# Scatter ahead of the own half, and ranks ahead of sums and x row, in eight steps of a fused attention and mixture-of-experts kernel

## The chip, the cores and the metric

The kernel runs on one core of a Trainium2 chip. The metric is the time of one execution in device microseconds; smaller is better. The core has the engines TensorE (PE in the profile, its weight loads as PEld), VectorE (DVE), ScalarE (ACT), GpSimd (POOL) and SyncE (SP), each with a queue of its own that is worked through in program order. They meet by semaphores.

## The reference

Windowed causal attention over 8 batches, 8 heads, 576 positions and 64 features is followed by a mixture of 8 experts, of which each token takes the one with the largest logit.

```python
scores = scale * np.matmul(q, k.transpose(0, 1, 3, 2))
mask = (rel >= 0) & (rel < 64)               # rel: query position - key position
scores = np.where(mask, scores, -1000000000.0)
attn = softmax(scores)                       # written out, with 1e-09 in the divisor
x = (attn @ v).transpose(0, 2, 1, 3).reshape(4608, 512)

logits = (x / |x|) @ (emb / |emb|).T / tau   # norms with 1e-06 added
expert_idx = np.argmax(logits, axis=1)
gate_w = softmax(logits)[arange(N), expert_idx]
for e in range(8):
    h = np.maximum(x[mask_e] @ w1[e], 0.0)   # 512 -> 1024
    out[mask_e] = gate_w * (h @ w2[e])       # 1024 -> 512
```

## The kernel before

The 4608 tokens are 36 tiles of 128 rows. A tile T holds two blocks of 64 positions for all heads. The order of all instructions is written out by hand. `stages(s)` (L580) writes step s of a software pipeline, and a loop calls it for s = 0 to 34; the last tile is written out behind it and is interleaved with the first expert's work.

In step s different tiles are in different states, and each engine works through its own part in this order:

- TensorE: `scores(s)` into the PSUM tile `score` (L255), in some steps the logits of four tiles (`logits_four`, L403), `values_other(s-2)` (L321), the transposes of the attention weights of tile s-1 (`attn_transposes`, L285), the transposes of x of tile s-3 (L378), in some steps the ranks of four tiles (`ranks`), and `values_mine(s-2)` (L335).
- ScalarE: `own_scores(s)` copies one half of the scores out (L262); in some steps half a weight tile is rounded to w1h (L599); `attn_copy(s-1)` (L295); the copy of x's transposes (L384); in some steps the copies of logits (L413, L416); squares; and at the end `exponentials(s)` (L276).
- VectorE: `all_scores(s)` (L265), `maxima(s)` (L269), in some steps the choice of the expert (L445 to L449), `attn_prev(s-1)` (L298), in some steps `rank_own` (L503), `x_out(s-2)`, which is sums, reciprocal and the x row (L359, L360, L363), then `ranks_out` (a reduction to the rows' places `pi`, L513), and in some steps the weight difference w1l = w1raw - w1h of 512 columns (L686).
- GpSimd: `less_max(s)` subtracts the maxima (L273), in some steps tokens and counts (L367, L457), `attn_own(s-1)` multiplies the own half of the attention weights with its mask (L301), and `place(T)` scatters the rows of a tile to the DRAM table `xs` at the places `pi` (an indirect DMA, L522).

`values_mine(s-2)` in step s reads what `attn_own(s-2)` wrote in step s-1. `scores(s+1)` may begin when `all_scores(s)` has read the PSUM tile.

Tiles come in groups of four (tiles 0 to 27) and of two. The ranks of a group of four that ends before tile b are worked out in step b+5, its tile T is scattered in step T+9. The weight difference is made in the eight steps of `wsplit`: 14, 17, 18, 21, 22, 25, 26 and 29. In 17, 21, 25 and 29 of these a group's ranks fall due, and the scatter of that step needs them. In the other four the places are known from the step before.

After step 30 SyncE's queue loads the first rows of `xs` for the experts (`load_x`, L899); VectorE transposes them in steps 32 and 33 (`x_turned`, L914), behind the x row of that step. From then on the experts' matmuls (L1032, L1093) follow one another on TensorE. There the weight differences are made at L201, x's at L930, and the output rows are scattered at L1121.

Of the kernel before, what the change touches and what calls it, by code (L numbers as in the profile page):

```python
# [33 lines left out]
GROUPS = [(t, t + 4) for t in range(0, 28, 4)] + [(t, t + 2) for t in range(28, 36, 2)]  # L34
# [90 lines left out]
def attention_moe(ctx, tc, q, k, v, emb, tau, w1, w2, kc, kt, out):  # L125
# [14 lines left out]
    def weave(*chains):  # L140

        chains = list(chains)
        while chains:
            chains = [c for c in chains if next(c, chains) is not chains]
# [83 lines left out]
    def scores(T):  # L228

        for z in range(2):  # L230
            if (2 * T + z) % NB == 0:
                for hp in range(2):
                    o = score[64 * z:64 * z + 64, hp].rearrange("p (u c) -> p u c", u=4)[:, :, :WIN]
                    nc.tensor.matmul(o, lhsT=ones[64 * hp:64 * hp + 64, :64],
                                     rhs=low[64 * hp:64 * hp + 64].rearrange("p (u c) -> p u c", u=4),
                                     start=True, stop=True)
        at = T % RK * KT
        for u in range(4):
            for hp, z in sides:
                pr, o = slice(64 * hp, 64 * hp + 64), score[64 * z:64 * z + 64, hp, u * P:(u + 1) * P]  # L240
                qz = qT[pr, T % RQ, u, z * WIN:(z + 1) * WIN]
                own = kT[pr, at + u * P + z * WIN:at + u * P + (z + 1) * WIN]
                if (2 * T + z) % NB == 0:
                    parts = [(o[:, WIN:], own)]
                elif z:
                    parts = [(o, kT[pr, at + u * P:at + (u + 1) * P])]
                else:
                    was = (T - 1) % RK * KT + u * P + WIN
                    if at:
                        hop = KT - WIN  # L250
                        parts = [(o, kT[pr, was:was + 2 * hop].rearrange("p (a c) -> p a c", a=2)[:, :, :WIN])]
                    else:
                        parts = [(o[:, :WIN], kT[pr, was:was + WIN]), (o[:, WIN:], own)]
                for to, keys in parts:
                    nc.tensor.matmul(to, lhsT=qz, rhs=keys, start=True, stop=True)  # L255
# [4 lines left out]
    def own_scores(T):  # L260
        sm[T] = ap.tile([P, 4, 2, WIN], F32, name="sm", bufs=3)
        nc.scalar.copy(sm[T], sv[:, :, :, 1])  # L262
# [17 lines left out]
    def attn_transposes(T):  # L280

        pT[T] = back.rearrange("p (u c) -> p u c", u=4)
        t = sm.pop(T).rearrange("p u h c -> p u (h c)")
        for u in range(4):
            nc.tensor.transpose(pT[T][:, u], t[:, u], ident)  # L285
# [7 lines left out]
    def attn_copy(T):  # L293
        aM[T] = ap.tile([P, 2, 4, P], F32, name="aM", bufs=2)
        nc.scalar.copy(aM[T][:, 0], pT[T])  # L295
# [4 lines left out]
    def attn_own(T):  # L300
        nc.gpsimd.tensor_tensor(out=aM[T][:, 0], in0=aM[T][:, 0], in1=halves[:, 0].unsqueeze(1).to_broadcast([P, 4, P]), op=ALU.mult)  # L301
# [197 lines left out]
    def rank_own(G):  # L499
        a, b = GROUPS[G]  # L500
        n = b - a
        rk = rkb[G] = ap.tile([P, n, E], F32, name="rk")
        nc.vector.tensor_tensor(out=rk, in0=rank.pop(G), in1=ohs.pop(G), op=ALU.mult)  # L503

    def rank_rows(G):
        a, b = GROUPS[G]
        n = b - a
        if G not in rkb:
            rank_own(G)
            yield  # L510
        rks[G] = ap.tile([P, n], I32, name="pi")
        with nc.allow_low_precision("whole numbers"):
            nc.vector.reduce_sum(out=rks[G], in_=rkb.pop(G), axis=AX.X)  # L513
        yield

    def ranks_out(G):
        weave(rank_rows(G))

    def place(T):

        i = T - GROUPS[OF[T]][0]
        d = nc.gpsimd.indirect_dma_start(  # L522
            out=xs[:, :], out_offset=bass.IndirectOffsetOnAxis(ap=rks[OF[T]][:, i:i + 1], axis=0),
            in_=xr.pop(T), in_offset=None, bounds_check=TBL - 1, oob_is_err=False)
        d = getattr(d, "ins", d)
        for o in firsts:
            tc.declare_no_dep(d, o, reason="later tokens' places are behind the early slots")
        for o in puts:
            tc.declare_no_dep(d, o, reason="no two tokens share a place")
        puts.append(d)  # L530
# [42 lines left out]
    wsplit = {s0: (i // 2, slice(i % 2 * 512, i % 2 * 512 + 512)) for i, s0 in enumerate((14, 17, 18, 21, 22, 25, 26, 29))}  # L573

    def warm(n, to=back):

        for _ in range(n):
            nc.tensor.matmul(to[:, :P], lhsT=ones, rhs=ones, start=True, stop=True)

    def stages(s):  # L580

        def there(d):
            return 0 <= s - d < NT

        def ending(d):
            return [G for G, (a, b) in enumerate(GROUPS) if b + d == s]

        def turned():
            if there(1):
                attn_transposes(s - 1)  # L590
                attn_copy(s - 1)

        scores(s)
        if s < 3:
            warm(12, side[1])
        own_scores(s)
        if s in wsplit:
            c, at = wsplit[s]
            nc.scalar.copy(w1h[c][:, at], w1raw[c][:, at])  # L599
        if 0 < s <= 3:  # L600
            exponentials(s - 1)
        if s == 33:
            x_hi(0)
        four = [G for G in ending(3) if len(range(*GROUPS[G])) == 4]
        for G in four:
            logits_four(G)
            four_copy(G)
        load_q(s + RQ)
        if there(2):
            values_other(s - 2)  # L610
        load_v(s + RV - 3)
        for f in wsteps.get(s, ()):
            f()
        if s > 3:
            turned()
        if there(3):
            x_transposes(s - 3)
        for G in four:
            four_back(G)
        if s - 4 in (28, 29):  # L620
            logits(s - 4, side[(s + 1) % 2][:, :E])
        due = [G for G, (a, b) in enumerate(GROUPS) if s == (b + 5 if b - a == 4 else b + 4)]
        for G in due:
            if len(range(*GROUPS[G])) == 4:
                ranks(G)
        if there(2):
            values_mine(s - 2)
        all_scores(s)
        maxima(s)
        late = [G for G in ending(4) if len(range(*GROUPS[G])) == 4]  # L630
        for G in late:
            choose(G)
        if s < 3:
            warm(12, side[1])
        if there(3):
            xT_evac(s - 3)
        for G in four:
            four_out(G)
        if s - 4 in (28, 29):
            nc.scalar.copy(x_rows(s - 4, s - 3)[:, 0, C_LOG:C_LOG + E], side[(s + 1) % 2][:, :E])  # L640
        less_max(s)
        if there(3):
            squares(s - 3)
        for G in four:
            four_beside(G)
        load_k(s + RK - 1, nc.sync if s < 6 else nc.scalar)
        for G in late:
            tokens(G)
            count(G)
        if s > 3:  # L650
            attn_prev(s - 1)
            attn_own(s - 1)
        for G in due:
            if len(range(*GROUPS[G])) == 4:
                rank_own(G)
        if there(2):
            x_out(s - 2)
        if s in (32, 33):
            x_turned(s - 32)
        if 0 < s <= 3:  # L660
            turned()
            attn_prev(s - 1)
            attn_own(s - 1)
        for G in due:
            if len(range(*GROUPS[G])) == 2:
                ranks(G)
            ranks_out(G)
        for G, (a, b) in enumerate(GROUPS):
            for T in range(a, b):
                if s == (T + 9 if b - a == 4 else b + 4):  # L670
                    place(T)
        if s == 33:
            x_lo(0)
        for G in ending(3):
            if len(range(*GROUPS[G])) == 2:
                choose(G)
                tokens(G)
                count(G)
        if s > 2:
            exponentials(s)  # L680
        if s == 33:
            x_hi(1)
            x_lo(1)
        if s in wsplit:
            c, at = wsplit[s]
            nc.vector.tensor_tensor(out=w1l[c][:, at], in0=w1raw[c][:, at], in1=w1h[c][:, at].bitcast(F32), op=ALU.subtract)  # L686
        if 1 <= s < 7:
            blanks(s - 1)
# [588 lines left out]
    T, G = NT - 1, len(GROUPS) - 1  # L1277
# [201 lines left out]
```

## Time and profile before

| | |
|---|---|
| Median of 3 runs | 608.63 us (607.76 to 610.57) |
| Profiled execution | 604.64 us, its span 602.9 us |
| TensorE busy | 580.4 us, 96% of the span |
| VectorE busy | 368.3 us, 61% |
| ScalarE busy | 292.8 us, 49% |
| GpSimd busy | 243.0 us, 40% |
| Granted TensorE clock, mean | 0.996 |
| Bytes moved | 110.11 MB, mean 183 GB/s |

Times in the rows are microseconds from the start of the span. In a timeline row stand the start, the duration, the engine, the line of the kernel, the operation, what it writes and reads, and in brackets the idle time ahead of it on its engine with what ended that. Consecutive instructions of an engine overlap by up to about 0.1 us at their ends, so a start of the next one may lie ahead of the end of the last. TensorE's ends are modelled.

### The profile page before, as it was taken

The page shows a single profiled execution, that of the slowest core. Times are in us where ns is not written, and L with a number is a line of the kernel's source. Part 1 is how long each engine was busy: PE and PEld are TensorE (multiplying, and loading weights), DVE is VectorE, ACT ScalarE, POOL GpSimd, SP SyncE. Part 2 cuts the span into 40 slices and gives each one's busy share as a digit, 9 for nine tenths or more (in the row PEclk, how much of TensorE's full clock was granted, in tenths as well). Part 3 has the DMA queues.
Part 4 walks back from the last instruction along what each step waited for, and adds up shares of the span by engine and source line. Part 5 has one row for each costly group of instructions (what it writes and reads, how often), then busy time and mean ns, then how long its engine had stood idle before and what let it go on. Part 6 is the DMA issues. An engine that isn't in the chain of part 4 may idle for free.

```text
span 602.9 us, 16141 instructions
## 1 busy us (share of the span) xinstructions
PE 580.4 (96%) x6198; PEld 500.2 (83%) x6198; DVE 368.3 (61%) x880; ACT 292.8 (49%) x519; POOL 243.0 (40%) x230
## 2 busy tenths in 40 slices
PE   8998899999999999999999999999999999999995
PEld 7887788788889888888888888888888999989984
DVE  5787889988589766166066166156255473728583
ACT  3676777777441465155145145235344363436362
POOL 3657878887822433314215115105204233113221
PEclk9999999999999999999999999999999999999998
DMA  8988889886334787743544454445336355556820
GB/s 282 301 257 268 285 258 297 262 274 189 136 112 173 206 273 221 201 126 126 168 148 127 138 151 157 110 155 184 89 122 207 117 158 144 177 177 174 241 91 23
DMA packets 72471, 110.11 MB, mean 183 GB/s; under 512 B 14773, under 2 KB 34997, under 8 KB 72384
## 3 DMA queue, kind: packets, MB, share of 16 engines
q1 hardware_dynamic: 62080, 80.88, 46.0%
q0 software_dynamic: 6000, 19.18, 8.2%
q10 hardware_dynamic: 4304, 8.93, 4.6%
q8 instruction: 50, 0.82, 0.6%
q14 instruction: 37, 0.30, 0.1%
HBM read 89.69 MB, written 20.05 MB: 182 GB/s over the span
## 4 chain that ended last, share of the span: by engine, by line
PE 76%; DVE 7%; issue 6%; DMA 3%; POOL 3%; ACT 2%; SPq 0%; POOLq 0%; ACTq 0%; DVEq 0%
PE ph L1032 35%; PE po L1093 33%; DMA out<-o,rest 2%; DVE sm L265 2%; DVE aM L298 2%; PE back L285 1%; POOL sm L273 1%; PE odd L335 1%; PE score L255 1%; POOL aM L301 1%; PE odd L321 1%; DVE st L269 1%; PE even L335 1%; PE xback L378 1%; ACT sm L262 1%
## 5 line engine op out<-in xcount | busy, mean ns | idle before, releaser
L1053 DVE SCALAR_TENSOR_TENSOR hl<-ph,hh 128x512 fp32r<-128x512 f32 (+2 forms) x84 | 54.2, 648 | 154.6 <-ACT hh L1049 154.6
L1032 PE MATMUL ph<-xh,w1h 128*128 128x512 f32 (+2 forms) x384 | 132.7, 345 | 1.3 <-DVE rk L503 1.3
L1032 PE MATMUL ph<-xl,w1h 128*128 128x512 f32 (+2 forms) x384 | 132.1, 344 | 0.0
L1032 PE MATMUL ph<-xh,w1l 128*128 128x512 f32 (+2 forms) x384 | 132.1, 344 | 0.0
L930 POOL TENSOR_TENSOR xl<-xt,xh 128x512 fp32r<-128x512 f32 x37 | 61.7, 1668 | 166.1 <-ACT xh L926 165.8
L1093 PE MATMUL po<-w2l,hh 128*128 128x512 f32 x312 | 121.8, 390 | 0.6 <-DVE w2l L201 0.5
L1093 PE MATMUL po<-w2h,hh 128*128 128x512 f32 x312 | 122.0, 391 | 0.0
L1093 PE MATMUL po<-w2h,hl 128*128 128x512 f32 x312 | 121.7, 390 | 0.0
L1049 ACT ACTIVATE hh<-ph 128x512 fp32r<-128x512 f32 (+2 forms) x84 | 47.4, 566 | 133.2 <-PE ph L1032 121.6
L1121 POOL DMA_INDIRECT out<-o,rest x39 | 43.0, 1101 | 132.3 <-ACT o L1118 107.1
L1032 PEld LDWEIGHTS ph<-xh,w1h 128*128 128x128 f32 x384 | 72.1, 188 | 9.1 <-issue 1.4
L1032 PEld LDWEIGHTS ph<-xl,w1h 128*128 128x128 f32 x384 | 72.2, 188 | 7.9 <-POOL xl L930 0.2
L1032 PEld LDWEIGHTS ph<-xh,w1l 128*128 128x128 f32 x384 | 72.1, 188 | 7.5
L1093 PEld LDWEIGHTS po<-w2l,hh 128*128 128x128 f32 x312 | 58.6, 188 | 13.2 <-DVE w2l L201 1.5
L1093 PEld LDWEIGHTS po<-w2h,hl 128*128 128x128 f32 x312 | 58.6, 188 | 12.3
L1093 PEld LDWEIGHTS po<-w2h,hh 128*128 128x128 f32 x312 | 58.6, 188 | 11.9
L201 DVE TENSOR_TENSOR w1l<-w1raw,w1h 128x1024 fp32r<-128x1024 f32 x44 | 60.3, 1378 | 9.9 <-ACT w1h L198 9.9
L201 DVE TENSOR_TENSOR w2l<-w2raw,w2h 128x1024 fp32r<-128x1024 f32 x48 | 58.8, 1225 | 11.8 <-ACT w2h L198 11.8
L1118 ACT ACTIVATE o<-po,gate 128x512 f32<-128x512 f32 (+1 forms) x39 | 26.4, 683 | 52.3 <-PE po L1093 46.9
L198 ACT CAST w2h<-w2raw 128x1024 fp32r<-128x1024 f32 x48 | 50.1, 1043 | 0.0
L273 POOL TENSOR_TENSOR sm<-sm,st 128x512 f32<-128x512 f32 x36 | 37.3, 1037 | 30.3 <-DVE st L269 22.6
L198 ACT CAST w1h<-w1raw 128x1024 fp32r<-128x1024 f32 x44 | 45.7, 1044 | 2.8 <-DMA w1raw<-in_w 2.8
(225 smaller groups left out, 823.2 us busy)
## 6 DMA issues: line engine op xcount, KB each, us to landing
w2raw<-in_w SPq DMA_DIRECT2D x44, 512.0 KB, 4.1
w1raw<-in_w SPq DMA_DIRECT2D x40, 512.0 KB, 3.8
xb<-xs SPq DMA_DIRECT2D x156, 64.0 KB, 3.2
v<-in_v SPq DMA_DIRECT2D x36, 260.0 KB, 4.9
qT<-in_q SPq DMA_DIRECT2D x36, 256.0 KB, 4.7
kT<-in_k ACTq DMA_DIRECT2D x26, 256.0 KB, 4.4
kT<-in_k SPq DMA_DIRECT2D x10, 256.0 KB, 5.1
w1raw<-in_w SPq DMA_DIRECT2D x8, 256.0 KB, 4.8
```

What stands on the lines that cost most here:

```text
L198: nc.scalar.copy(hi[c], raw[c])
L201: eng.tensor_tensor(out=lo[c], in0=raw[c], in1=hi[c].bitcast(F32), op=ALU.subtract)
L265: nc.vector.copy_predicated(sm[T], sel.unsqueeze(1).unsqueeze(1).to_broadcast([P, 4, 2, WIN]), sv[:, :, :, 0])
L273: nc.gpsimd.tensor_tensor(out=t, in0=t, in1=st.pop(T).unsqueeze(2).to_broadcast([P, 8, WIN]), op=ALU.subtract)
L298: nc.vector.tensor_tensor(out=aM[T][:, 1], in0=pT.pop(T), in1=halves[:, 1].unsqueeze(1).to_broadcast([P, 4, P]), op=ALU.mult)
L930: eng.tensor_tensor(out=xl, in0=t, in1=xh.bitcast(F32), op=ALU.subtract)
L1032: nc.tensor.matmul(o, lhsT=ww[c][:, f * P:(f + 1) * P], rhs=xx[:, c, :n], start=(c == 0 and i == 0), stop=(c == 3 and i == 2))
L1049: nc.scalar.activation(hh, ph[g, part][:, :parts(g) * rows_of(g)], AF.Relu)
L1053: nc.vector.scalar_tensor_tensor(out=hl, in0=ph.pop((g, part))[:, :parts(g) * rows_of(g)], scalar=0.0, in1=hh.bitcast(F32), op0=ALU.max, o ...
L1093: nc.tensor.matmul(o, lhsT=xx, rhs=ww[f // 2][:, f % 2], start=(f == 0 and k == 0), stop=(f == 7 and k == 2))
L1118: nc.scalar.activation(o[:, :w], y[:, :w], AF.Copy, scale=gate[:, at:at + 1])
L1121: d = nc.gpsimd.indirect_dma_start(out=out, out_offset=bass.IndirectOffsetOnAxis(ap=tok, axis=0), in_=o, in_offset=None, bounds_check=N - ...
```

## The change

In the eight steps of `wsplit` three things move within `stages(s)`; in all other steps the order stays.

- `place`, the scatter of a tile's rows, is called ahead of `attn_own(s-1)` instead of behind `x_out`, the two-tile groups and `ranks_out`. On GpSimd's queue the scatter so stands between `less_max` and the own half. The loop over tiles that called it becomes a function `places(s)`.
- Where a group's ranks fall due in such a step (17, 21, 25, 29), `ranks_out`, the reduction to places, follows right behind `rank_own`, ahead of `x_out`'s sums and x row on VectorE's queue.
- `attn_own(s-1)` is called behind both.

No instruction is added or removed.

```diff
+    def places(s):
+
+        for G, (a, b) in enumerate(GROUPS):
+            for T in range(a, b):
+                if s == (T + 9 if b - a == 4 else b + 4):
+                    place(T)
...
         if s > 3:
             attn_prev(s - 1)
-            attn_own(s - 1)
         for G in due:
             if len(range(*GROUPS[G])) == 4:
                 rank_own(G)
+                if s in wsplit:
+                    ranks_out(G)
+        if s in wsplit:
+            places(s)
+        if s > 3:
+            attn_own(s - 1)
         if there(2):
             x_out(s - 2)
...
         for G in due:
             if len(range(*GROUPS[G])) == 2:
                 ranks(G)
-            ranks_out(G)
-        for G, (a, b) in enumerate(GROUPS):
-            for T in range(a, b):
-                if s == (T + 9 if b - a == 4 else b + 4):
-                    place(T)
+            if len(range(*GROUPS[G])) == 2 or s not in wsplit:
+                ranks_out(G)
+        if s not in wsplit:
+            places(s)
```

## Rows read from the trace of the kernel before

**Rows 1.** The page's first part: busy us (share of the span) and instructions.

```profile
PE 580.4 (96%) x6198; PEld 500.2 (83%) x6198; DVE 368.3 (61%) x880; ACT 292.8 (49%) x519; POOL 243.0 (40%) x230
```

**Rows 2.** Windows of steps 21, 22, 23, cut at `less_max`: length, busy times, clock, DMA.

```profile
94.86:99.20 4.34, 4.32 (x140) 3.94 (x144) 4.17 (x10) 3.72 (x9) 3.47 (x3) 1.00 0.93 315
99.20:103.55 4.35, 4.35 (x124) 3.68 (x118) 4.18 (x8) 2.85 (x8) 3.55 (x4) 1.00 0.91 263
103.55:107.36 3.81, 3.41 (x110) 3.10 (x104) 2.98 (x7) 2.76 (x8) 3.27 (x3) 1.00 0.97 311
```

**Rows 3.** Single lines: count, ns shortest/median/longest, first and last start.

```profile
L686 DVE TENSOR_TENSOR w1l<-w1raw,w1h x8: 1168/1264/1375, 65.9 to 130.0; 128x512 fp32r<-128x512 f32 x8
...
L930 DVE TENSOR_TENSOR xl<-xt,xh x2: 683/684/684, 177.2 to 177.8; 128x512 fp32r<-128x512 f32 x2
...
L522 POOL DMA_INDIRECT xs<-xr,pi x28: 972/1014/1959, 46.2 to 182.4; - x28
```

**Rows 4.** Timeline of VectorE and GpSimd in steps 21 and 22.

```profile
95.86 1.27 POOL L301 TENSOR_TENSOR aM<-aM,cs 128x512 f32<-128x512 f32 x1
...
96.42 0.17 DVE L513 TENSOR_REDUCE pi<-rk 128x4 int32<-128x32 f32 x1
...
96.51 1.17 DVE L686 TENSOR_TENSOR w1l<-w1raw,w1h 128x512 fp32r<-128x512 f32 x1
...
100.21 1.27 POOL L301 TENSOR_TENSOR aM<-aM,cs 128x512 f32<-128x512 f32 x1
...
100.66 1.37 DVE L686 TENSOR_TENSOR w1l<-w1raw,w1h 128x512 fp32r<-128x512 f32 x1
...
101.64 1.27 POOL L522 DMA_INDIRECT xs<-xr,pi  x1 [0.16 <-issue]
```

**Rows 5.** Timeline in the experts: a scatter, and VectorE's difference inside it.

```profile
326.43 1.04 POOL L1121 DMA_INDIRECT out<-o,rest  x1 [0.17 <-issue]
...
326.74 1.23 DVE L201 TENSOR_TENSOR w1l<-w1raw,w1h 128x1024 fp32r<-128x1024 f32 x1 [0.85 <-ACT w1h L198]
```

**Rows 6.** Timeline of ScalarE at the end of step 23: `own_scores(24)`.

```profile
105.15 0.57 ACT L262 COPY sm<-score 128x512 f32<-128x512 f32 x1
```

**Rows 7.** Timeline of TensorE: `values_mine(20)` and `scores(24)`.

```profile
97.63 1.05 PE L335 MATMUL even<-v,aM 64*128 64x65 f32 x24
...
103.28 1.13 PE L255 MATMUL score<-kT,qT 64*64 64x128 f32 x32
```

**Rows 8.** Timeline of steps 25 to 27: TensorE behind the shift, ScalarE ahead of the exponentials.

```profile
114.39 0.66 PE L378 MATMUL xback<-cs,xmore 128*128 128x128 f32 x4 [0.29 <-DVE shift L491]
114.98 1.06 PE L335 MATMUL even<-v,aM 64*128 64x65 f32 x24
...
120.83 0.21 ACT L416 COPY odd<-even 128x32 f32<-128x32 f32 x1
121.55 0.63 ACT L276 ACTIVATE sm<-sm 128x512 f32<-128x512 f32 x1 [0.51 <-POOL sm L273]
```

**Rows 9.** Steps 15 to 19: timeline of `values_mine(13)`, two stops in the chain, ScalarE's copy.

```profile
68.10 0.62 PE L335 MATMUL odd<-v,aM 64*64 64x65 f32 x13
...
72.86 1.75 issue
...
83.56 0.85 issue
...
87.74 0.21 ACT L416 COPY odd<-even 128x32 f32<-128x32 f32 x1
```

**Rows 10.** Timeline of steps 30 to 33: `values_mine(28)`, `x_turned(0)`, the end of `values_mine(31)`, its sums.

```profile
131.15 1.06 PE L335 MATMUL even<-v,aM 64*128 64x65 f32 x24
...
143.17 0.89 DVE L914 STREAM_TRANSPOSE xt<-xb 128x128 f32<-128x128 f32 x4
...
145.26 0.22 PE L335 MATMUL odd<-v,aM 64*64 64x65 f32 x2
...
146.09 0.16 DVE L359 TENSOR_SCALAR sums<-odd 128x8 f32<-128x8 f32 x1
```

## What the change should do, worked out before its time was known

> **What bounds the kernel now.** I read the busy shares first, then a table of the attention steps by windows, then the timeline of each engine inside two of the changed steps, then the chain of waits, and last the hand-over to the experts. TensorE is busy 96% of the span, VectorE 61%, GpSimd 40% [rows 1]: so time is gained only where TensorE waits for others, and that is in the 35 attention steps, before about 150 us; behind them the experts run on TensorE alone. A step is counted here from one `less_max` to the next. A plain step takes 3.81 us (step 23), the changed steps 21 and 22 take 4.34 and 4.35 [rows 2]; eight of the 35 are changed (14, 17, 18, 21, 22, 25, 26, 29).
>
> A plain step is a ring: `less_max(23)` at 103.55, exponentials, `own_scores(24)` at 105.15 (1.60 later), `all_scores(24)`, the maxima, and the next `less_max` at 107.36 [rows 2, 6]. In a changed step VectorE is the longer way round, since the weight difference w1l lies ahead of the next `all_scores` (VectorE busy 4.18 of 4.35 in step 22, [rows 2]). But TensorE is as full: 4.32 of 4.34 and 4.35 of 4.35 in steps 21 and 22 [rows 2]. That second number decides this prediction.
>
> **Why w1l is long.** It takes 1.17 to 1.38 us, median 1.26, where the same subtraction of 512 columns from SBUF takes 0.684 on VectorE with GpSimd idle [rows 3]. In step 21 the own half (L301) runs 95.86 to 97.13 and w1l, begun at 96.51, ends at 97.68, 0.55 after it. In step 22 the own half ends at 101.48 and w1l at 102.03, again 0.55 after. So w1l stands still until the own half is done. The scatter behind it, begun at 101.64 inside w1l, takes 1.27 instead of a median of 1.01 [rows 3, 4].
>
> **What the change does, part by part.**
>
> Scatter ahead of the own half. After `less_max` GpSimd now issues the scatter (1.01, with 0.16 of gap ahead of it, as between 101.48 and 101.64) and then the own half. What it costs beside w1l isn't shown in the changed steps themselves, since there w1l always begins first. The nearest row is in the experts: an output scatter from 326.43 to 327.47, and a subtraction of 1024 columns that begins inside it at 326.74 and takes 1.23, less than twice 0.684 [rows 3, 5]. So a subtraction that begins inside a scatter isn't held. I take 0.68 for w1l; the other bound is that it waits for the scatter's end (below). The saving on VectorE is 1.17 - 0.68 = 0.49 in the four steps with ranks and 1.37 - 0.68 = 0.69 in the others, 4.7 us in all.
>
> The Trainium skill ("SBUF — State Buffer", section "Who interferes with whom") says that VectorE's tensor_tensor with two SBUF inputs and a GpSimd instruction that reads SBUF exclude each other for the whole instruction, whoever begins first; by that rule the pair w1l and own half behaves as the rows have it. The same section infers that descriptor generation needs only the write side and isn't stalled by a tensor_tensor; the scatter of 1.27 speaks against that. If the exclusion held for scatters both ways, the result would be the third rival.
>
> Ranks ahead of sums and x row (steps 17, 21, 25, 29). The reduction of 0.17 (L513, [rows 4]) moves ahead of the sums. It now follows at once on the product that it reads, while in the old place other work lay between: between nothing and its own 0.17 of VectorE's time [rows 4]; I take 0.1 as an estimate. It leaves 0.40 of the 0.49. The scatter's new wait for it costs nothing: in step 21 the ranks would be ready about 0.8 before their 96.59 of now, and `less_max` ends at about 95.88, where the own half behind it starts now. Behind the waiting scatter stand the own half and the next `less_max`.
>
> The own half is late. Step 21: `less_max` from 94.86, scatter about 96.1 to 97.1, own half from 97.2 to about 98.5; before it ended at 97.13. GpSimd itself still has room: the next `less_max` is due at 98.8. But `values_mine(20)` on TensorE reads the own half and now begins at 97.63 [rows 7]. It would begin at 98.5, 0.87 later, and behind it on TensorE's queue stand the scores of step 23, the logits of four tiles and everything up to the scores of step 24. No DMA is moved on SP's or ScalarE's queue; the scatters go out about 1.3 us earlier on GpSimd's, and nobody waits for those of the eight steps.
>
> **Where the gain goes, group by group.** Steps 21 to 24: `all_scores(22)` comes 0.40 earlier. TensorE is full in step 22, so its 0.87 stay: the scores of step 24, 103.28 to 104.41 [rows 7], end at 105.28 and `own_scores(24)`, now 105.15 [rows 6], starts 0.15 later. VectorE had reached `less_max(23)` at about 102.9 and the ring would ask for `own_scores(24)` at 104.5; it finds no scores. Sum: +0.15.
>
> Steps 25 to 28: TensorE waits here anyway 0.29 for the shift (L491), so x's transposes come at 114.39 and `values_mine(24)` at 114.98 [rows 8]; the own half, done at about 115.0, costs it 0.1. The `less_max(27)` comes about 1 us earlier, but ScalarE has the logits' copies until 121.04 and then 121.14, and the exponentials of step 27, now at 121.55 [rows 8], go to about 121.17. Sum: -0.37.
>
> Steps 17 to 20: here TensorE has a stop of 0.85 at 83.56 with no releaser, in the logits, and the copies on ScalarE that follow from it end at 87.95, with the exponentials behind them [rows 9]. The late own half costs 0.87 just ahead of that stop and fills it; VectorE's gain dies at those copies. Sum: 0 (bounds: -0.7 if the stop shrinks, +0.85 if it moves with TensorE).
>
> Step 14: the own half would end at about 68.0 (its 1.27 behind the scatter), and `values_mine(13)` begins at 68.10 [rows 9], so nothing is late and up to its 0.69 are gained, but TensorE's stop of 1.75 at 72.86 [rows 9] comes two steps later. Bounds 0 and -0.69; I take 0, since that stop too has no releaser that the change moves.
>
> Step 29: VectorE gives 0.40 and with it the last scatter that the first expert's rows wait for; VectorE's transposes of those rows, at 143.17 after an idle wait, come that much earlier. But `values_mine(28)` goes from 131.15 to 132.0, and TensorE is nearly gapless from there to 145.48, the end of `values_mine(31)`, for which the sums at 146.09 wait next [rows 10]. With 0.22 of gain carried in (0.37 - 0.15) and 0.87 lost it ends at 146.13, where the sums stand now. Sum over all at the hand-over: 0.0 us. From there everything is shifted as a whole.
>
> So 4.7 us are taken from VectorE and none arrives: the profiled execution of 604.64 (span 602.9) stays at 604.6. The median of the runs before, 608.63, stands 4.0 above that execution; I take the same distance: **608.6 us**.
>
> **Rivals.** (1) VectorE's gain arrives: TensorE's queue has slack that the modelled ends of its matmuls hide, the late own half is covered, and the eight steps fall to about 3.82: 8 x 0.5 = 4.0, so 604.6; about half of it, 606.6, if the two stops keep theirs. For it: VectorE is the longest way in the changed steps; against: TensorE's 4.35 of 4.35 [rows 2]. (2) The late own half isn't covered: the stop at 83.56 moves with TensorE (+0.85), step 29's loss reaches the hand-over (+0.87 less its 0.2) and step 25 gives nothing: with +0.15 about +1.6, 610.2. It decides from the point where TensorE has less than 0.74 of slack ahead of `own_scores`, as in step 23. (3) The scatter holds w1l as the own half did: then w1l begins at 97.1 and ends at 97.7, as before, and the own half ends at 98.9, 1.7 late. No gain, and TensorE loses 1.3 in each of the four steps with ranks, of which 0.74, 0.85 and 0.3 are covered in three: about 0.55 + 0.45 + 0.1 + 1.0 = 2.1, so 610.7, and up to 611.7 where nothing covers the fourth or step 14. Against it: the 1.23 [rows 5]. (4) It doesn't do what it says, w1l stays above 1.1 for another neighbour: 608.6.
>
> **How the numbers follow.** Forecast, within 1 us of 608.6: 0.61. Rival 1: 0.15, half of it beyond 3.0 us. Rival 2: 0.14. Rival 3: 0.07. Rival 4: 0.03. A measurement of this kernel can tell about 0.5%, 3.0 us, from no change. Faster by more: 0.08, from rival 1. Slower by more: 0.06, from rivals 2 and 3 where their upper bounds add to a spread of runs like that of before (607.76 to 610.57). Same: 0.86. Range: the low end takes in half of rival 1, 606.0; the high end rival 2, 610.4.
>
> **What would show it.** w1l at about 0.68 in all eight steps and the scatter at 1.0 (else rival 3 or 4); `values_mine` of tiles 16, 20 and 28 about 0.85 later within their steps; steps 21 and 22 shorter by `less_max`, but step 23 longer (about 4.6 instead of 3.81); exponentials of step 27 earlier; the sums of tile 31 within 0.5 us of 146.1. It would be wrong if step 23 stayed at 3.81 with steps 21 and 22 at 3.85, or if TensorE showed pauses ahead of `values_mine` that end in pauses later in the same group.

## The result and the profile after

The kernel after takes 611.92 us in the median of 15 runs (609.26 to 616.59), the kernel before beside it 609.13 (606.79 to 613.95, 15 runs). The ratio is 1.0060, 95% interval 1.0036 to 1.0083: 0.6% slower; the median is 1.5 us above the upper end of the range forecast, 606.0 to 610.4. Here and below a ratio is taken over the fast runs, those not in a slower state of the chip, and is not the quotient of the two medians, which is 1.0046 here. The profiled execution after is 611.92, its span 610.1.

The page's busy times, to be held against [rows 1]:

```profile
PE 587.9 (96%) x6198; PEld 505.3 (83%) x6198; DVE 368.9 (60%) x880; ACT 293.5 (48%) x519; POOL 241.3 (40%) x230
```

Windows of steps 21 to 23 of the kernel after, cut at `less_max`, with the columns of [rows 2] (length; busy time and count of PE, PEld, DVE, ACT and POOL; granted clock, DMA share, GB/s):

```profile
94.26:98.23 3.97, 2.85 (x93) 2.47 (x92) 3.76 (x10) 3.06 (x7) 3.29 (x3) 1.00 0.97 339
98.23:103.82 5.59, 5.49 (x137) 4.64 (x137) 4.85 (x8) 3.22 (x9) 3.33 (x3) 1.00 0.82 251
103.82:107.65 3.83, 3.83 (x129) 3.54 (x129) 3.09 (x7) 3.35 (x10) 3.30 (x3) 1.00 0.84 259
```

w1l's line, with the columns of [rows 3]:

```profile
L697 DVE TENSOR_TENSOR w1l<-w1raw,w1h x8: 681/682/1946, 65.9 to 131.2; 128x512 fp32r<-128x512 f32 x8
```

Step 21 fell from 4.34 to 3.97, with TensorE busy 2.85 of it. Step 22 rose from 4.35 to 5.59. w1l's median is 0.68 instead of 1.26, but its longest is 1.95: six of the eight took 0.68, those of steps 18 and 22 1.95 and 1.94. VectorE's total is what it was.

The timeline of VectorE, GpSimd and TensorE in these two steps of the kernel after, in order of time (against [rows 4] and [rows 7]):

```profile
94.90 0.19 DVE L513 TENSOR_REDUCE pi<-rk 128x4 int32<-128x32 f32 x1
...
95.86 0.99 POOL L522 DMA_INDIRECT xs<-xr,pi  x1 [0.56 <-DVE sums L360]
96.04 0.68 DVE L697 TENSOR_TENSOR w1l<-w1raw,w1h 128x512 fp32r<-128x512 f32 x1
96.88 1.27 POOL L301 TENSOR_TENSOR aM<-aM,cs 128x512 f32<-128x512 f32 x1
98.20 1.06 PE L335 MATMUL even<-v,aM 64*128 64x65 f32 x24 [1.09 <-POOL aM L301]
...
99.32 0.17 DVE L359 TENSOR_SCALAR sums<-even 128x8 f32<-128x8 f32 x1 [0.57 <-PE even L335]
...
100.37 1.94 DVE L697 TENSOR_TENSOR w1l<-w1raw,w1h 128x512 fp32r<-128x512 f32 x1
100.47 1.28 POOL L301 TENSOR_TENSOR aM<-aM,cs 128x512 f32<-128x512 f32 x1
```

In step 21 the first half of the forecast comes true: w1l runs inside the scatter at its short time. But the own half ends at 98.15, and TensorE, idle for 1.09, begins `values_mine(20)` at 98.20. The sums of tile 20 wait 0.57 for that, so w1l of step 22 begins late, at 100.37, 0.10 ahead of that step's own half, and stands still beside it until 0.56 after its end (101.75 to 102.31). Step 21 gains 0.37, and step 22 loses 1.24.

Step 25 has a third collision that I had not looked for. An instruction of two columns on VectorE that starts the late count (L493) took 0.23. Timeline of the kernel before:

```profile
114.44 0.23 DVE L493 SCALAR_TENSOR_TENSOR before<-iota,shift,before 128x2 bf16<-128x2 f32 x1
```

After, it begins together with the own half and lasts 1.30, and the step takes 5.36 instead of 4.68. Timeline of the kernel after:

```profile
114.36 1.30 DVE L493 SCALAR_TENSOR_TENSOR before<-iota,shift,before 128x2 bf16<-128x2 f32 x1
...
114.36 1.27 POOL L301 TENSOR_TENSOR aM<-aM,cs 128x512 f32<-128x512 f32 x1
```

Step 31 takes 6.33 instead of 3.82. The first expert matmul, the hand-over, is at 155.74 instead of 152.49. Of the 7.2 us by which this span is longer than that of before, 3.25 lie ahead of the hand-over and 3.95 behind it, where the granted clock fell twice (last section).

### The profile page after: what moved, and what is told of

The parts are those of the page before. It is cut to its first block, busy times and chain, and to the rows that moved or that the text cites. A ratio compares the mean times of both kernels' runs of the same rounds, so it can differ in the third digit from the quotient of the medians.

```text
span 610.1 us, 16137 instructions
## 1 busy us (share of the span) xinstructions
PE 587.9 (96%) x6198; PEld 505.3 (83%) x6198; DVE 368.9 (60%) x880; ACT 293.5 (48%) x519; POOL 241.3 (40%) x230
## 4 chain that ended last, share of the span: by engine, by line
PE 78%; issue 6%; DVE 6%; DMA 3%; POOL 3%; ACT 2%; SPq 0%; POOLq 0%; ACTq 0%; DVEq 0%
PE ph L1043 35%; PE po L1104 32%; DMA out<-o,rest 2%; PE back L285 2%; PE odd L321 2%; PE odd L335 2%; POOL aM L301 1%; PE score L255 1%; DVE aM L298 1%; DVE sm L265 1%; PE even L335 1%; POOL xs L522 1%; PE xback L378 1%; DVE st L269 1%; PE xback L403 1%
## 5 line engine op out<-in xcount | busy, mean ns | idle before, releaser
L1043 PEld LDWEIGHTS ph<-xh,w1l 128*128 128x128 f32 x384 | 73.4, 191 | 7.5
```

The costliest lines, as they stand in the source:

```text
L1043: nc.tensor.matmul(o, lhsT=ww[c][:, f * P:(f + 1) * P], rhs=xx[:, c, :n], start=(c == 0 and i == 0), stop=(c == 3 and i == 2))
```

## The experiments

The runs came in four groups, each on one chip, another one each time, with runs of the kernel before between them: before took 607.48 in the first group (26 runs), 603.83 and 603.86 in the second and third (35 each), 607.76 in the fourth (32). Ratios are to before of the same group. All kernels are the kernel after with two tuples of steps: `rows_ahead`, where the scatter goes ahead of the own half, and `ranks_ahead`, where `ranks_out` goes ahead of the sums.

```diff
-                if s in wsplit:
+                if s in ranks_ahead:
                     ranks_out(G)
-        if s in wsplit:
+        if s in rows_ahead:
             places(s)
```

### First group: the change taken apart

`rows_ahead` and `ranks_ahead` by kernel: e1 all eight steps and (17, 21, 25, 29); e2 (14, 18, 22, 26) and none; e3 (17, 21, 25, 29) and the same; e4 none and (17, 21, 25, 29).

**The whole change again.** 

> The whole change once more, to see how often and where the granted TensorE clock falls to its lower level and how much of the time lies ahead of the experts' first matmul. Late-own-half theory: 1.005 of the kernel before, with w1l near 1.95 us in steps 18 and 22 each time and the first expert matmul 2 to 3.5 us later than before (152.5 us). Clock theory: the first expert matmul at most 1 us later, the rest from a fallen clock, so executions with a mean clock of 0.996 and above are as quick as those of the kernel before (ratio 1.000 to 1.002).

Measured 611.6 (609.74 to 614.47), ratio 1.0062 [1.0029, 1.0095]; w1l again 1.94 in steps 18 and 22, the hand-over at 155.03. The clock theory fails: the profile shows no fall, and the two runs at a mean clock of 0.996 took 610.25 and 610.28, where the median of before is 607.48.

**The four steps without ranks.** 

> Only the steps 14, 18, 22 and 26 have the scatter ahead of the own half; 17, 21, 25 and 29 are as in the kernel before. Late-own-half theory: in these four the matmuls that read the own half come behind the logits of four tiles and aren't late, so w1l takes 0.68 in them, each step loses up to 0.5 us, and the kernel is 1.5 to 2 us quicker than before, about 0.997. Ranks theory (the loss comes from the reduction and the wait on it): the same 0.997, since no ranks are moved. Clock theory: 1.000 to 1.005, as the clock falls for reasons at the hand-over. If any scatter ahead of the own half costs: 1.002 or more.

Measured 609.3, ratio 1.0023 [0.9998, 1.0048]. Each of the four steps took 3.81 with w1l at 0.68, and the hand-over came at 150.11, but the 0.997 expected did not come. Two falls of the clock stand in its profile (150 to 158 and 167 to 175). Whether these four steps cost something can't be told from this interval; the third group tries them again.

**The four steps with ranks.** 

> Only the steps with ranks (17, 21, 25, 29) are changed, scatter and ranks both; 14, 18, 22, 26 are as before. Late-own-half theory: values_mine of tiles 16, 20, 24, 28 waits about 1.1 us, w1l is 0.68 in the changed steps, not 1.95 in steps 18 and 22 (there the own half is first and done early): a loss of 0.5 to 2 us, 1.001 to 1.003. If the two sets of steps only lose together, by w1l of 18 and 22 behind the own half: 0.999 to 1.000. Ranks theory: like the whole change, 1.005.

Measured 612.88, ratio 1.0096 [1.0064, 1.0128]: more than the whole change. All three expectations lay lower. w1l was 0.69 and 0.68 in steps 18 and 22, with no collision there (step 25 took 5.36, as after), but the logits steps 19, 23 and 31 took 5.50, 5.56 and 6.37, each with a stop of TensorE of 0.34 to 0.39 just ahead of it that nothing in the trace released (of these stops more below).

**Ranks alone, scatter in its old place.** 

> Only the ranks come ahead of sums and x row in steps 17, 21, 25, 29; every scatter stays behind the own half. Late-own-half theory: VectorE loses 0.1 us in four steps, 1.000 to 1.001. Ranks theory: a loss of 1 us and more, 1.002 to 1.005. Clock theory: 1.000, unless the hand-over's phase alone moves the clock.

Measured 608.21, ratio 1.0016 [0.9993, 1.0039]: no difference to be seen. w1l took 1.05 in the rank steps. The loss of the first group hangs on the scatter ahead of the own half in the steps with ranks, where it needs the ranks ahead as well.

### Second group: the late own half, and what one profile hides

**Old order, no own half in steps 18 and 21.** In both this kernel and the next the mask is not applied there.

```diff
-        if s > 3:
+        if s > 3 and s not in (18, 21):
             attn_own(s - 1)
```

> The order of the kernel before; in steps 18 and 21 the own half (the masking of tiles 17 and 20 on GpSimd) is left out, so their rows of x differ and with them the routing: only the stretch up to the hand-over is to be read. The weight difference w1l has no own half beside it and should take 0.68 in steps 18 and 21 (1.3 and 1.17 before), without anything coming late. If VectorE's gain can arrive at all, steps 18 and 21 take 3.8 to 3.9 instead of 4.33 and 4.34 and the steps behind them (19, and 22 with 23) stay at 4.2 and 8.16: 0.9 us in all. If TensorE is the bound there, as my prediction had it, the steps 18 with 19 and 21 with 22 and 23 keep their sums of before within 0.2, since what VectorE gains is waited for on TensorE.

w1l took 0.68 in both steps, step 18 3.88 and step 21 3.96. TensorE had stops that nothing in the trace released, 0.58 at 84.64 and 1.69 at 100.81, so the sums of the steps behind (4.42; 5.13 and 4.75) say nothing either way: inconclusive.

**The change in steps 18 and 21, no own half there.** 

> The change in steps 18 and 21 alone, and there the own half is left out as in the run of the old order without it. Theory (the late own half is what costs): with no own half to come late, values_mine of tile 20 stands without the idle 1.1 ahead of it, and step 23 is 3.8 to 4.2, not 5.56 as with the scatter ahead of the own half in the rank steps; steps 21 to 23 sum within 0.3 of the old order without own half, 12.1 to 12.5 in place of 13.9. Rival (the scatter itself, its wait of 0.56 for the ranks ahead of the next less_max, or its earlier transfer, is what costs): steps 21 to 23 stay near 13.5 to 13.9 though no own half is late, and values_mine or the logits of step 23 are late all the same.

Windows of steps 21, 22 and 23 of this kernel:

```profile
91.99:96.04 4.05, 4.02 (x129) 3.65 (x133) 3.84 (x10) 3.48 (x8) 2.02 (x2) 1.00 0.90 315
96.04:100.39 4.35, 4.35 (x124) 3.68 (x118) 4.18 (x8) 2.86 (x9) 3.55 (x3) 1.00 0.88 290
100.39:104.29 3.90, 3.72 (x116) 3.24 (x108) 3.08 (x7) 2.89 (x8) 3.28 (x3) 1.00 0.91 279
```

And `values_mine(20)` in step 21, from the timeline of TensorE in this kernel:

```profile
94.77 1.06 PE L335 MATMUL even<-v,aM 64*128 64x65 f32 x24
```

The three steps sum to 12.30, against 12.50 in [rows 2] and 13.39 after. Steps 18 and 19 sum to 7.71 against 8.16 in the old order without stops (e7 below). The scatter stood ahead, with its idle 0.57 in step 21, and nothing was lost; `values_mine(20)` came 2.78 behind `less_max(21)`, as before (2.77), and TensorE was busy 4.02 of step 21 instead of 2.85. So it is the own half behind the scatter that costs, not the scatter's place or its wait by itself, and some of VectorE's gain arrives where nothing comes late. Without an own half there is no collision on VectorE either; this run can't tell that from the lateness on TensorE, f3 below can.

**The old order with TensorE filled.** 20 small matmuls with an unused result stand in TensorE's idle time ahead of the first expert.

```diff
+    warm(20)
     layer1(0, 0)
```

> The order of the kernel before, with 20 small matmuls (128x128 bf16, result unused) in front of the first expert's matmul, where TensorE is idle for 1.26. They tell whether that idle time is what lets the granted clock fall to 0.50 behind the hand-over, as in the profiles of the change (155.9 to 159.9) and of the other four steps alone (151 to 156.5), though not in that of before. If it is: no fall there in the profile, mean granted clocks of the runs rise by about 0.003, the median falls by 1 to 2 us, ratio 0.997 to 0.999. If the falls come from elsewhere: falls at 152 to 157 in some executions as ever, ratio 1.000.

Measured 603.2 (602.33 to 605.08, 12 runs), ratio 0.9974 [0.9945, 1.0003]. All its runs had a mean granted clock of 0.996 or more; in this group 17 of the 35 runs of before were below 0.996, at 603.4 to 612.9 us.

**The kernel before once more.** 

> The kernel before once more, with the same instructions in the same order, for a second profile: TensorE's stops without a releaser (1.34, 1.75 and 0.85 in the first profile, of which the last two lie in steps 16 and 19) and the falls of the clock. If those are of an execution and not of the kernel, they stand elsewhere here or have other sizes; step 16 is then about 4.1 instead of 5.23 and step 19 about 3.8 to 4.0, the hand-over is at about 150, and the 2.4 us by which the other four steps alone came earlier to it are stops of the one profile and no gain. If they belong to the kernel before, they stand again in steps 16 and 19 and the hand-over is at 152.5. Ratio 1.000 +- 0.003.

Ratio 0.9988 [0.9948, 1.0027]. Its TensorE timeline at two stops, in the scores during step 16 and in the logits ahead of step 19:

```profile
75.56 0.98 PE L255 MATMUL score<-kT,qT 64*64 64x128 f32 x25 [0.59 <-issue]
...
84.82 0.41 PE L403 MATMUL xback<-xfour,embT 128*32 128x128 f32 x4 [0.30 <-issue]
```

In the first profile of before the stops at the same instructions were 1.75 and 0.85 [rows 9]; in the filled old order neither is there. These two return at the same instructions in other sizes. But e8 also has stops of 1.66 at 55.89 and 0.73 at 105.21, in the scores, and its step 23, with the second of them, took 4.46 instead of 3.81. Step 16 took 4.16 instead of 5.23, step 19 3.82 instead of 4.24. So e2's early hand-over was mostly the stops of the profile that I had compared it with: from step 14 to the hand-over it took 86.66 (1.29 of stops in it), before 88.03, but the filled old order, which has none there, 86.14.

### Third group: the three orders on filled ground

All four have `warm(20)`; f0 is e7's order once more, f1, f2 and f3 have the tuples of e1, e2 and e3.

> The kernel before with the 20 small matmuls ahead of the first expert's, once more, as the ground on which the three orders that follow can be compared without falls of the clock. If the idle time of 1.27 ahead of the experts is what the clock falls after: all runs within 3 us of one another at a mean granted clock of 0.996 or more, and a median 0.5 to 2 us below that of before; ratio 0.997 to 0.999. If the narrow spread of the first filled run (602.33 to 605.08) was chance, it spreads like before.

> The whole change on the same ground. Theory: the loss lies in the attention steps (from step 14 to the hand-over 91.3 in two profiles of the change against 86.1 in the old order without a stop), so it is no smaller without falls: 4 to 5 us above the filled old order, ratio to it 1.006 to 1.009, and again w1l of 1.94 in steps 18 and 22 and step 31 of 6.3. Rival (a good part of the loss was the falls of the clock at 155.9 and 172 in the profile of the change): not more than 2 us above it.

> The scatter ahead of the own half in steps 14, 18, 22 and 26 alone, on the same ground. Theory: each gives its own step 0.5 (w1l 0.68, step 3.81) and takes 0.5 to 0.9 from the next, where TensorE is late behind the late own half; from step 14 to the hand-over 86 to 87, time within 1 us of the filled old order (ratio 0.999 to 1.002). Rival (the gain of 2 us in the attention steps is real, and only the falls behind the hand-over hid it): 2 us below the filled old order, ratio 0.9965.

> Scatter and ranks ahead in steps 17, 21, 25 and 29 alone, on the same ground. Theory: here the own half is 2 us late, with the scatter's wait for the ranks ahead of it, and TensorE, idle 1.1 ahead of values_mine, makes none of it good in steps 19, 23 and 31 (5.5, 5.55 and 6.37); 5 to 7 us above the filled old order, more than the whole change, ratio 1.008 to 1.012. Rival (the two halves of the change cost independently, so that each is less than the whole): below the whole change.

| | f0 old order | f1 whole change | f2 other four | f3 rank steps |
|---|---|---|---|---|
| median us (range, 12 runs each) | 603.43 (602.35 to 606.59) | 605.49 (604.10 to 606.38) | 603.47 (601.47 to 606.99) | 605.84 (604.01 to 608.88) |
| ratio to before | 0.9988 [0.9961, 1.0015] | 1.0015 [0.9992, 1.0038] | 0.9989 [0.9961, 1.0018] | 1.0025 [1.0000, 1.0050] |
| steps 14 to 16 | 12.26 | 12.75 | 11.82 | 12.26 |
| steps 17 to 20 | 16.61 | 17.48 | 16.25 | 16.92 |
| steps 21 to 24 | 16.60 | 17.48 | 17.31 | 16.96 |
| steps 25 to 28 | 16.92 | 17.36 | 16.66 | 17.63 |
| steps 29 to 31 | 11.99 | 12.80 | 12.00 | 12.79 |
| stops in these steps | none | 0.52 (step 14) | 1.10 (step 22), 0.35 (step 29) | none |

f0's spread is 4 us, wider than e7's. The change costs 2.06 us here in the medians (eight of f0's twelve runs lie below f1's lowest), less than my theory's 4 to 5 and just beyond the rival's 2, and its step 31 is 4.63, not 6.3. f3 costs 2.41, below its 5 to 7 and about as much as the whole. By steps 14 to 31, less the stop of 0.52, f1 loses 2.97 and f3 2.18. From the hand-over to the end the four profiles take 449.9 to 450.3, so the loss lies ahead of it.

f2 costs nothing in the medians (0.04), as the theory had it, but the theory's reason fails: the step behind took 0.13 to 0.27 more where it has no stop (steps 15, 19 and 27: 3.94, 4.00 and 4.08 against 3.81, 3.83 and 3.81), not 0.5 to 0.9. Its profile keeps 0.44, 0.36 and 0.26 in the three groups of steps without the stop of 1.10. So a part of VectorE's gain arrives in the steps without ranks, though TensorE is busy 4.35 of 4.35 in step 18 of f0 as well. Why the median shows nothing of it was not tried.

How a late own half becomes a longer ring is cleanest in f3, where no stop and no collision is near. Its windows of steps 21 to 23:

```profile
93.72:97.70 3.98, 2.85 (x92) 2.48 (x92) 3.77 (x10) 3.42 (x8) 3.29 (x4) 1.00 1.00 322
97.70:102.05 4.35, 4.35 (x128) 3.84 (x129) 3.52 (x7) 1.99 (x6) 3.56 (x3) 1.00 0.71 255
102.05:106.60 4.55, 4.55 (x135) 4.08 (x136) 3.27 (x7) 4.06 (x11) 3.28 (x3) 1.00 0.96 302
```

From its timeline, TensorE and ScalarE in these steps:

```profile
97.66 1.05 PE L335 MATMUL even<-v,aM 64*128 64x65 f32 x24 [1.10 <-POOL aM L301]
...
102.09 0.27 PE L410 MATMUL even<-cs,lT 128*128 128x128 f32 x1
...
103.51 0.21 ACT L416 COPY odd<-even 128x32 f32<-128x32 f32 x1
103.85 0.63 ACT L276 ACTIVATE sm<-sm 128x512 f32<-128x512 f32 x1
```

Step 23 of the filled old order, f0, by its window:

```profile
102.69:106.51 3.82, 3.42 (x108) 3.05 (x104) 2.98 (x7) 2.72 (x8) 3.28 (x3) 1.00 0.95 313
```

and by its timeline:

```profile
101.31 0.27 PE L410 MATMUL even<-cs,lT 128*128 128x128 f32 x1
...
102.73 0.21 ACT L416 COPY odd<-even 128x32 f32<-128x32 f32 x1
103.76 0.63 ACT L276 ACTIVATE sm<-sm 128x512 f32<-128x512 f32 x1 [0.83 <-POOL sm L273]
```

In f0 ScalarE waits 0.83 for `less_max(23)` and begins its exponentials 1.07 behind that one's start. In f3 `values_mine(20)` is late, TensorE runs without a gap through step 22 (4.35 of 4.35), so the transpose of the logits (L410) is late too, ScalarE's copies of them (L413 to L416) reach past the point at which `less_max(23)` is ready, and the exponentials come 1.80 behind its start: 0.73 later, which is what the step has more, 4.55 against 3.82. Step 21's gain is 0.36. In f3 too the late sums begin w1l of step 22 late, but there the own half stands first on GpSimd and is nearly done (99.98) when w1l begins (99.83), and w1l takes 0.70. In f1 the late sums push w1l into the own half instead, and step 22 takes 5.59.

### Fourth group: why the loss was larger in the first runs

> The kernel before on the chip of this two by two. Both theories: ratio 1.000. Its profile gives the stops without a releaser and the falls of the clock on this chip: with many stops of 0.3 to 0.5 behind step 30 and from 0 to 20 us behind the hand-over, it is a chip like that of the first four runs; with none, like that of the last eight.

> The whole change, unfilled. Falls of the clock are the rest: 3.5 us or more above the old order unfilled (ratio 1.006) while the filled change is 2 above the filled old order, and its runs spread to 612 at clocks below 0.993. Stops of the chip are the rest: the same difference as between the two filled ones, within 0.8 us; 2 us with step 31 at 4.6 where the chip has few stops, 3.5 us with step 31 at 6.3 where it has many.

> The old order with the 20 matmuls ahead of the experts, a third time. If the idle time ahead of the experts lets the clock fall, its runs again lie close together at clocks of 0.996 or more, and its median 0.4 to 0.8 us below the unfilled one; else no difference.

> The whole change with the 20 matmuls. Falls of the clock are the rest: 2.0 to 2.5 us above the filled old order (1.0035) whatever the unfilled pair shows. Stops of the chip are the rest: the same difference as in the unfilled pair within 0.8 us, 3.5 us where the chip has many stops.

| | old order | whole change | difference |
|---|---|---|---|
| unfilled | 608.00 (ratio 1.0008 [0.9987, 1.0029]) | 613.03 (1.0071 [1.0045, 1.0097]) | 5.0 |
| filled | 607.88 (0.9985 [0.9959, 1.0012]) | 611.71 (1.0063 [1.0037, 1.0088]) | 3.8 |

So the fill does not take the loss away, and where before is at 607.8 it is larger, 3.8 filled against 2.1 in the third group. The falls of the clock are not the rest of it; between filled and unfilled 1.2 us remain (the bound that I had set was 0.8), but by the means of the same runs the two differences are 3.95 and 3.91. What differs between the groups is seen in step 31 of the same program: 6.37 in g3, 4.63 in f1. TensorE and ScalarE in steps 30 and 31 of g3:

```profile
138.62 0.47 PE L321 MATMUL odd<-v,aM 64*64 64x65 f32 x13 [0.33 <-issue]
138.74 0.27 ACT L407 COPY lT<-xback 128x128 f32<-128x128 f32 x1 [1.29 <-PE xback L403]
...
141.04 1.05 PE L255 MATMUL score<-kT,qT 64*64 64x128 f32 x32
...
143.19 0.35 PE L321 MATMUL even<-v,aM 64*64 64x65 f32 x4 [0.40 <-issue]
143.24 0.59 ACT L262 COPY sm<-score 128x512 f32<-128x512 f32 x1 [1.13 <-PE score L255]
```

and of f1:

```profile
136.61 0.27 ACT L407 COPY lT<-xback 128x128 f32<-128x128 f32 x1 [0.50 <-PE xback L403]
...
139.02 1.05 PE L255 MATMUL score<-kT,qT 64*64 64x128 f32 x32
...
140.14 0.59 ACT L262 COPY sm<-score 128x512 f32<-128x512 f32 x1
```

In f1 `own_scores` (L262) starts at 140.14, just behind the modelled end of the scores (140.07). In g3 the scores end by the model at 142.09, but the copy starts at 143.24, just behind a stop of TensorE that the trace shows as 0.40 in the next group of matmuls. I read this as the stop costing its readers 1.1. With the stop of 0.33 ahead of them the scores start 1.94 into step 31 instead of 1.26. Together 1.76, and step 31 is 1.74 longer: about what the filled loss differs by between the groups (3.8 and 2.1). Stops of 0.30 to 0.45 at these two places stand in the profiles of the whole change from the result, the first and the fourth group (four of four), and not in f1. The old order of the fourth group has none there in g2 and one of 0.45 at another matmul of step 31 in g0; its step 31 is 3.82 in both. Why the late TensorE of the change meets them and the old order doesn't was not tried and stays open, as does what TensorE waits for in them.

Nor does every execution of the change have the same collisions. In g1, with a stop of 0.83 in step 17 (4.79 long), w1l of step 18 took 0.68 and that step 3.83. In g3 step 14 has one (5.56 instead of 3.82 in f1). From g3's timeline:

```profile
65.98 0.99 POOL L522 DMA_INDIRECT xs<-xr,pi  x1 [0.16 <-issue]
66.43 2.40 DVE L700 TENSOR_TENSOR w1l<-w1raw,w1h 128x512 fp32r<-128x512 f32 x1
67.00 1.27 POOL L301 TENSOR_TENSOR aM<-aM,cs 128x512 f32<-128x512 f32 x1
```

w1l began inside the scatter, 0.57 ahead of the own half. At 0.68 it would have ended at 67.11; the own half began at 67.00, and w1l ended at 68.83, 0.56 behind it. In f1 it began 0.27 behind the start of the scatter instead of 0.45, and ended 0.07 ahead of the own half. So the new order leaves w1l a gap with little to spare.

## Why the prediction was wrong

**Right:** the reading of w1l as held by the own half, and the scatter not holding it (0.68 in six steps, scatter 0.99 to 1.01); that a late TensorE costs in the steps with ranks; rival 3 excluded. The sign of step 21's own half was right, its lateness too small: I had `values_mine` 0.87 late, and in time from `less_max(21)` it went from 2.77 to 3.94, 1.17. The sign of step 23 (about 4.6) came true in f3 (4.55), not in the kernel after (3.83), where step 22 is long instead.

**Wrong, by step of the prediction.** The loss comes from the second of these: where the late own half goes, which I had priced at +0.15 and 0.

- "The scatter's new wait for it costs nothing." The places were written by 95.09, before `less_max` ended at 95.29, as I had it; yet the scatter began at 95.86, 0.56 idle instead of 0.16. That 0.40 goes straight onto the own half. The same idle time stands in all four steps with ranks (0.56 or 0.57), where the scatters of most other steps have 0.15 or 0.16. The trace names the reciprocal of the sums (L360) as the releaser, 0.47 after its end; whether it is that wait or the release itself was not told apart.
- "Steps 21 to 24: +0.15", "steps 17 to 20: 0". Both were +0.88 and +0.87 in f1 against f0. I followed the late TensorE to `own_scores(24)` alone. It goes two other ways first: over the logits' copies on ScalarE to the exponentials (+0.73 in step 23 of f3), and over the sums of `x_out`, which read what `values_mine` writes, to the place of w1l in the next step, where it meets the next own half (1.94 for 0.68). I had used the first way in steps 25 to 28, and not in 21 to 24; the second is missing from the prediction altogether. (My 102.9 for `less_max(23)` takes only step 22's 0.69 off 103.55; with step 21's 0.40 it is about 102.5, which changes nothing in a sum that waits for the scores.)
- "Steps 25 to 28: -0.37." It was +0.44. The -0.37 needed step 25 no longer than before; L493 (0.23) fell beside the own half and took 1.30. I gave each VectorE instruction its new time but asked only of w1l what GpSimd does beside it.
- "Step 29 and the hand-over: 0.0". Steps 29 to 31 were +0.81, step 31 alone +0.81 (4.63 against 3.82), the same late logits (in f1 the exponentials begin 1.68 behind `less_max(31)`, in f0 1.06); step 29 gained 0.37 and step 30 lost as much. The sums of tile 31, forecast within 0.5 of 146.1, came at 149.33.
- "Step 14: 0" came out near the number, by luck. f1 has +0.49 in steps 14 to 16 with a stop of 0.52 in it. f2, with the same order in these steps and no stop, has -0.44; and the stop of 1.75 that was to swallow the gain is neither in f0 nor in f1 or f2.
- "4.7 us are taken from VectorE and none arrives." In the four steps without ranks a part arrives, by f2's profile 0.26 to 0.44 for each. TensorE's 4.35 of 4.35, the number that was to decide, did not rule that out; rival 1 holds for these steps in part.
- The 608.6 leaned on three runs of before. Before measured 609.13 beside the change, so 0.5 of the 3.3 us by which the forecast fell short is that.

Rival 2, the late own half not covered, is what happened, at about twice its price: +1.6 forecast, +2.97 by steps and 2.1 in time on the one chip, 3.8 on the other. I gave it 0.14, since I let the lateness end wherever the profile of before showed a wait: 0.74 ahead of `own_scores`, the stop of 0.85, the logits' copies. Two of these covers were none: the stop changes with the execution (0.85 there, 0 to 0.70 in the profiles since), and the copies are late by the same TensorE. In the steps with ranks, what came late to a TensorE that was busy 4.35 of 4.35 stayed late.

## What to carry to other kernels

Moving an instruction behind another is paid by whoever reads its result: follow the late result through every engine that waits for it, around the ring, until it meets the moved step again, and not only to the end of the current step. When two engines hold each other up, list every instruction that the new time puts side by side, not the one pair that the change is about. Before a step's length is put into a sum, take a second profile of the same kernel: what stands without a releaser may have another size in the next execution.

## What the runs showed of the hardware

**Which instructions are held.** w1l that began and ended inside a scatter took 0.68 (scatter 0.99 to 1.01). w1l that began 0.10 ahead of the own half on GpSimd took 1.94, w1l that began 0.57 ahead of it (g3, step 14) 2.40, and an instruction on only two columns took 1.30 beside it. By the starts in the trace, being first by 0.10 or 0.57 did not help VectorE's instruction; GpSimd's went through at its usual 1.27 or 1.28, and w1l ended 0.55 to 0.56 behind it, in the old order as in the new.

**The clock and the idle time at the hand-over.** Windows of the kernel after: the hand-over's idle time, what follows, and a later stretch.

```profile
151.90:155.90 4.00, 2.61 (x79) 2.23 (x79) 3.61 (x10) 2.08 (x6) 3.78 (x6) 0.99 0.21 82
155.90:159.90 4.00, 4.00 (x44) 3.61 (x44) 0.00 (x0) 2.05 (x3) 3.53 (x5) 0.59 0.01 4
...
172.00:176.90 4.90, 4.54 (x28) 4.53 (x29) 4.13 (x12) 0.00 (x0) 0.37 (x3) 0.65 0.42 119
```

The granted clock is 0.59 and 0.65 there (1.2 of 2.4 GHz for most of each stretch), the first just behind 1.27 of idle TensorE. The same idle time in the profiled execution of before (1.26 ahead of 152.49) was followed by no fall. None of the seven profiles with the 20 matmuls in the idle time has a fall between 140 and 164; of the eleven without them four have one (after, e2, e4, e5). A later fall came with them too (g2, at 170 to 174, behind two stops of 0.34 and 0.38; in g3 two of 0.29 and 0.38 were followed by none), and filled runs with mean clocks down to 0.991 stand in f2 and g2. So that the idle time is the cause of the fall is suggested, not shown. In time the fill gave ratios of 0.9974, 0.9988 and 0.9985, but the interval reaches past 1 each time: no gain is shown.
